# Single-bank PSUM tiles for the last batch, landing times in the planner, and token loads spread over the units

## The chip, the core and the metric

The kernel runs on one core of a Trainium2 chip. The metric is the device time of one execution in microseconds (us); the number quoted is the median of three runs. A profiled execution, taken apart from these runs, gives the trace. Engines are named as in the trace: PE (TensorE matmuls), PEld (its weight loads), DVE (VectorE), ACT (ScalarE), POOL (GpSimd), SP (SyncE, whose queue issues every DMA of this kernel; SPq in the rows).

## The reference

Three layers follow each other. Arrays are fp32.

```python
def _attn_ref(x, state):                     # x (4, 8, 512, 64), state (4, 8, 32, 64)
    scores = scale * np.matmul(x, state.transpose(0, 1, 3, 2))
    a = softmax(scores)                      # over the 32 state rows
    xread = np.matmul(a, state)
    a2 = softmax(scale * np.matmul(state, x.transpose(0, 1, 3, 2)))
    sread = np.matmul(a2, x)
    return np.concatenate([xread, sread], axis=2)

def _moe_ref(x, w_in, w_out):                # 2176 tokens, 512 -> 2048 -> 512
    h = x @ w_in
    g = np.where(h >= 1, h, np.where(h <= -1, 0.0, (h + 1) ** 2 / 4))
    return g @ w_out

def _moe2_ref(x, w_a, w_b, w_out):           # 512 -> 1536 -> 512
    return ((x @ w_a) * (x @ w_b)) @ w_out
```

(`softmax` stands here for the max, exp, sum and division of the reference.) The 2176 tokens are 4 batches of 512 and 128 state rows.

## The kernel before

**Arithmetic.** PE multiplies in a short format, so an fp32 operand is split into a high part, which ACT writes (a copy into `rh`, `r`, `r0` or `r1`), and a low part, which DVE writes (a subtraction, L356). Each product is then three passes: high by high, high by low, low by high. The three large matmuls (`g @ w_out`, the pair `x @ w_a`, `x @ w_b`, and the last one) are done with seven block products instead of eight, called by their numbers (in `b_steps` in the order 1, 2, 5, 3, 6, 7, 4). Sums of blocks are made by DVE (L900) before a product, and finished products are added up by ACT copies and DVE adds that read PSUM.

**Stages.** `phase_one` runs 64 units, t = 0 to 63: unit t is batch t // 16 and one slice of 128 of the 2048 middle columns. A unit is 6 matmuls of 512 columns into one PSUM bank (`h_mm`, L371), then its gate: ACT takes the ReLU out of the bank into an SBUF buffer `g` (L779), ACT or POOL squares it (L786, L788), DVE clamps it and so reads the bank a second time (L793), and SP stores it to DRAM, array `g_d` (L337). Between units 47 and 48 four groups of `h_state` matmuls (L825) do the state rows in the same way. The next stage, `b_steps`, multiplies `g` by `w_out`: it loads tokens of `g_d` back (L334, `f1<-g_d` and `f0<-g_d`, each 128x2x368), splits them and runs the seven products of each of three chunks of tokens, each product into two banks. Its first steps are taken between the last units, so that units and products are mixed there. `ab_run` then makes the two factors of the last layer (stored as `p_d`, L337), and `o_run` reads `p_d` back in pieces of 128x6x256 and makes the output, run after run.

**Banks.** PSUM has 8 banks of 512 fp32 words. Banks 0 to 3 are single tiles. Banks 4, 5 and banks 6, 7 are each one tile of 1024 words, because the attention's steps read both at once. The tile framework keeps its waits per tile, so an engine that reads bank 6 waits for a write of bank 7 before it in the program, and the other way round. Units 0 to 47 take banks 0 to 3 in turn (`four`), units 48 to 63 take 4, 5, 6, 7, 2, 3, again 4, 5, 6, 7, 2, 3, and then 6, 7, 2, 3 (`six`). In `b_steps` products 2 and 5 alone use banks 4 to 7, with product 3 adding onto product 5's banks 6 and 7. The buffers `g` of units 48 to 63 are a ring of six (`qlast`), so unit 54 writes the buffer of unit 48 once its store has landed.

**The order of the work.** One planner, `Flow`, puts the whole program in an order. Each operation has a cost per engine that may do it, its dependences, and for a transfer its size. `order()` walks through a modelled time: per step it takes the engine and the operation that can start first, PE's own in program order. `fin[i]` is when a result is usable; for a transfer it is when it lands (its share of one modelled wire and `DMA_LAT` behind it). `free[e]` is when the engine can issue its next operation. `when[s]`, the earliest start of a successor, is `free[e]` if both run on the same engine, else `fin[i]`. All transfers are on SP, so a load that reads what a store writes counts as ready once the store is issued, though on the chip SP waits there until it has landed, and every transfer behind it in the queue waits too. `STARTS` lists at which unit each of the first 17 steps of `b_steps` begins; the first 12 are the token loads of one piece each, which the line `flow.gate = units[-1]` ties to the unit before.

Of the kernel before, what the change touches and what calls it, by code (L numbers as in the profile page):

```python
# [9 lines left out]
F32 = mybir.dt.float32  # L10
F32R = mybir.dt.float32r
U32 = mybir.dt.uint32
AF = mybir.ActivationFunctionType
ALU = mybir.AluOpType
AX = mybir.AxisListType
PSUM = bass.MemoryType.PSUM
# [3 lines left out]
class Flow:  # L20
# [64 lines left out]
    def order(self):  # L85
        ops = self.ops
# [48 lines left out]
        for _ in range(n):  # L135
            best = None
            for e, f in free.items():
                x = None
                if e == "PE" and at < len(chain) and not left[chain[at]]:
                    i = chain[at]  # L140
                    x = (max(f, when[i]), 1e9, i, e)
                soon = min((max(f, when[i]) for i in ready[e]), default=0.0)
                soon += self.SOON if soon < self.EARLY else 0.0

                z = None
                for i in ready[e]:
                    t = max(f, when[i])
                    if t <= soon:
                        y = (late[i], t, i)
                        z = min(z, y) if z else y  # L150
                if z:
                    y = (z[1], z[0], z[2], e)
                    x = min(x, y) if x else y
                if x:
                    best = min(best, x) if best else x
            if best is None:

                raise RuntimeError("nothing is ready")
            t, _, i, e = best
            start[i] = t  # L160
            free[e] = t + ops[i][0][e]
            if i in self.port and e in shared:
                other = shared["POOL" if e == "DVE" else "DVE"]
                free[e] += min(max(other - t, 0.0), ops[i][0][e])
                shared[e] = free[e]
            if i in ideal:
                at += 1
                lag = max(lag, t - ideal[i])
            else:
                for x in ops[i][0]:  # L170
                    ready[x].remove(i)
            fin[i] = free[e] + self.LAT[e]
            if ops[i][3]:
                wire = max(wire, free[e]) + ops[i][3] / self.DMA_RATE
                fin[i] = wire + self.DMA_LAT
            for s in after[i]:
                left[s] -= 1
                when[s] = max(when[s], free[e] if (e,) == (*ops[s][0],) else fin[i])
                if not left[s]:
                    offer(s)  # L180
            self.ops[i] = (*ops[i][:4], e)
# [5 lines left out]
def attention_then_two_mlps(  # L187
# [28 lines left out]
    SWITCH = 48  # L216
    HOLD = 1
    FILL = (12, 10)
    STARTS = (48, 48, 49, 49, 50, 50, 51, 51, 52, 53, 54, 55, 56, 57, 59, 61, 62)
    HALVES = 1  # L220
    TIMES = ((0, 3, 4, 5), (8, 10, 12, 18), (22, 24, 26, 34), (38, 40, 42, 0))
    RUSH = (4, 8, 4, 4)
# [81 lines left out]
    def bank(b):  # L304
        return ("P", b, b + 1)
# [23 lines left out]
    def t_mm(n, passes=1):  # L329
        return passes * max(n / 2400 + 0.0135, 0.112)  # L330
# [30 lines left out]
        hi_of(hi, src, n, regs(src), regs(hi) + list(also))  # L361
        tt(lo, src, lambda: hi(F32), ALU.subtract, n, regs(src, hi), regs(lo))

    def mms(b, cols, pairs, first, last, n, rd, onto=False, off=0):


        def emit(e):
# [4 lines left out]
                    o, w, x, start=first and k == 0, stop=last and k == n - 1, skip_group_check=onto  # L372
                )

        return op({"PE": n * t_mm(cols)}, emit, rd, [bank(b)])

    def three(w, x):

# [70 lines left out]
    arenas["R0"] = pc.tile([P, RLO // 4], F32R, name="r0")  # L449
    arenas["F0"] = pc.tile([P, F0 // 4], F32, name="f0")  # L450
    banks = [ps.tile([P, 512], F32, name=f"bank{b}") for b in range(4)]
    lower, upper = (ps.tile([P, 1024], F32, name=f"bank{b}") for b in (45, 67))
    banks += [lower[:, :512], lower[:, 512:], upper[:, :512], upper[:, 512:]]
    both = [("P", 4, 6)]
    spare = pc.tile([P, 1], F32, name="spare")
    g_d = pd.tile([F1, P, T], F32, name="g_d")
# [79 lines left out]
    def b_soft(b):  # L536
# [9 lines left out]
                port=True,  # L546
            )

        op({"DVE": 1.25}, lambda e: nc.vector.transpose(t1(), lower), both, regs(t1))
        op({"DVE": 1.22}, lambda e: nc.vector.reduce_max(mx(), b32w(t1()), axis=AX.X), regs(t1), regs(mx))  # L550
        spread(ALU.subtract, mx)
        act(t1, t1, 1024, AF.Exp, regs(t1), regs(t1), scale=SCALE)
# [97 lines left out]
    def w_steps(b, n, f0=0, f1=4):  # L650
# [26 lines left out]
        for q in [range(2)] if WIDE and cols == 4 * P else [range(1), range(1, 2)]:  # L677
            k, at = len(q), wsum[n][q[0]][0].at + 4 * P * f0
            hi, lo = (V2("R0", at + 2048 * h, k, 1024, cols) for h in range(2))
            src = lambda q=q: upper.rearrange("p (q c) -> p q c", q=2)[:, q[0] : q[-1] + 1, :cols]  # L680
            held = [bank(6 + i) for i in q]
            steps.append(lambda hi=hi, src=src, held=held, k=k: hi_of(hi, src, k * cols, held, regs(hi)))
            steps.append(
# [6 lines left out]
    def s_soft(b):  # L690
# [1 line left out]
        a2, sm = d["a2"], d["sm"].sub(64, 16)  # L692
        op(
            {"DVE": 1.22},
            lambda e: nc.vector.reduce_max(sm()[:, 0:2], lower.rearrange("p (q c) -> p q c", q=2), axis=AX.X),
            both,
            regs(sm),
        )
# [36 lines left out]
    def s_tr(b):  # L735
        d = bs[b]
        for q in range(2):
# [5 lines left out]
                    nc.tensor.transpose(banks[4 + q][:, r], v()[:, r], ident)  # L743

            op({"PE": 0.5}, emit, regs(v), [bank(4 + q)], loose=True)
        act(d["a2t"], lambda: lower, 1024, AF.Copy, both, regs(d["a2t"]))

    def s_read(b):
        d = bs[b]
# [20 lines left out]
    four, six = Ring([0, 1, 2, 3]), Ring([4, 5, 6, 7, 2, 3] * 2 + [6, 7, 2, 3])  # L770

    begun = {}
    units, first_w = [], []

    def gate(b, g, put):
        h = lambda: banks[b]
# [22 lines left out]
    def h_mm(j, f, cs=range(2)):  # L799
# [7 lines left out]
            return out  # L807

        used = [v.sub(P * o, P) for q in cs for v in wsum[n][q]] + [v for q in cs for v in att[2 * j + q]]
        units.append(mms(b, 512, pairs, cs[0] == 0, cs[-1] == 1, 3 * len(cs), regs(*used)))  # L810
        if cs[-1] < 1:
            begun[j, f] = b
            return
# [679 lines left out]
    with tc.manual_schedule():  # L1493
        nc.vector.memset(half, 0.5)
        nc.scalar.activation(spare, half, AF.Exp)
        make_identity(nc, ident)
        pool = tc.tile_pool(name="fs", bufs=1)
        arenas["FS"] = pool.__enter__().tile([P, FSB // 4], F32, name="fs")
        for i in order:
            if i == first_rh[0]:  # L1500
                pool.__exit__(None, None, None)
                del arenas["FS"]
# [9 lines left out]
            flow.ops[i][1](flow.ops[i][4])  # L1512
        pool.__exit__(None, None, None)
        high.__exit__(None, None, None)


# [46 lines left out]
```

## Time and profile before

| | |
|---|---|
| median of 3 runs | 731.68 us (731.52 to 732.62) |
| profiled execution, its own time | 737.83 us |
| its span, first to last instruction | 735.0 us |
| PE busy / PEld busy | 706.0 us (96%) / 658.3 us |
| DVE / ACT / POOL busy | 554.6 / 422.2 / 104.7 us |
| mean granted TensorE clock | 0.991 |
| chain that ended last | PE 78%, DMA 9%, DVE 6%, ACT 3% |

A share of busy time is a mean over stages. Times in the rows below are microseconds from the start of the span; the profiled execution's time is its span and 2.83 us around it. In a row of a timeline the bracket is the idle time of the engine just ahead of the work, and whose work ended it.

### The profile page before, as it was taken

The page shows a single profiled execution, that of the slowest core. Times are in us where ns is not written, and L with a number is a line of the kernel's source. Part 1 is how long each engine was busy: PE and PEld are TensorE (multiplying, and loading weights), DVE is VectorE, ACT ScalarE, POOL GpSimd, SP SyncE. Part 2 cuts the span into 40 slices and gives each one's busy share as a digit, 9 for nine tenths or more (in the row PEclk, how much of TensorE's full clock was granted, in tenths as well). Part 3 has the DMA queues.
Part 4 walks back from the last instruction along what each step waited for, and adds up shares of the span by engine and source line. Part 5 has one row for each costly group of instructions (what it writes and reads, how often), then busy time and mean ns, then how long its engine had stood idle before and what let it go on. Part 6 is the DMA issues. An engine that isn't in the chain of part 4 may idle for free.

```text
span 735.0 us, 12233 instructions
## 1 busy us (share of the span) xinstructions
PE 706.0 (96%) x4818; PEld 658.3 (90%) x4818; DVE 554.6 (75%) x699; ACT 422.2 (57%) x623; POOL 104.7 (14%) x76
## 2 busy tenths in 40 slices
PE   7789899998999999999999999999999998999997
PEld 6356576987999999999999999999999998999997
DVE  6897769977898587789899786655636787978760
ACT  4787878777544445656566675655425445444440
POOL 3356546975000000000000000000000000000000
PEclk9999999999999999999999999999999999999999
DMA  9858867486557048125334767453541348345201
GB/s 344 355 196 274 312 210 279 145 302 212 183 189 280 21 122 253 57 85 173 100 122 169 261 186 241 154 176 132 190 147 41 109 140 274 101 146 171 85 33 43
DMA packets 75449, 128.92 MB, mean 175 GB/s; under 512 B 5632, under 2 KB 51200, under 8 KB 75392
## 3 DMA queue, kind: packets, MB, share of 16 engines
q1 hardware_dynamic: 75392, 128.15, 52.0%
q8 instruction: 37, 0.61, 0.3%
q14 instruction: 20, 0.16, 0.1%
HBM read 84.87 MB, written 43.25 MB: 174 GB/s over the span
## 4 chain that ended last, share of the span: by engine, by line
PE 78%; DMA 9%; DVE 6%; ACT 3%; issue 2%; POOL 1%; SPq 1%; ACTq 0%; POOLq 0%; DVEq 0%
PE bank L371 73%; DMA f<-in_w_dram 4%; PE bank L825 2%; DMA p_d<-f 1%; DMA f<-p_d 1%; ACT f L346 1%; DMA f<-g_d 1%; DVE r L356 1%; DMA g_d<-f 1%; PE bank L758 1%; DVE rh L356 1%; PE bank L660 1%; PE bank L849 1%; DVE fs L434 1%; DVE f L793 1%
## 5 line engine op out<-in xcount | busy, mean ns | idle before, releaser
L371 PE MATMUL bank<-rh,r 128*128 128x352 f32 (+2 forms) x1398 | 225.0, 316 | 4.8 <-ACT f L346 3.8
L371 PEld LDWEIGHTS bank<-rh,r 128*128 128x128 f32 x1398 | 216.2, 189 | 8.0 <-ACT f L346 5.9
L371 PE MATMUL bank<-r,r 128*128 128x368 f32 (+1 forms) x960 | 158.1, 317 | 3.5 <-ACT f L346 3.4
L346 ACT ACTIVATE f<-bank 128x368 f32<-128x368 f32 (+3 forms) x183 | 82.2, 453 | 130.4 <-PE bank L371 129.7
L371 PEld LDWEIGHTS bank<-r,r 128*128 128x128 f32 x960 | 149.4, 190 | 4.2 <-ACT f L346 4.2
L346 ACT ACTIVATE rh<-f 128x736 fp32r<-128x736 f32 (+4 forms) x120 | 100.4, 846 | 77.5 <-PE bank L371 62.1
L356 DVE TENSOR_TENSOR f<-bank,f 128x368 f32<-128x368 f32 (+2 forms) x168 | 85.8, 517 | 73.9 <-PE bank L371 63.8
L356 DVE TENSOR_TENSOR rh<-f,rh 128x736 fp32r<-128x736 f32 (+5 forms) x120 | 115.5, 973 | 27.5 <-ACT rh L346 27.1
L371 PE MATMUL bank<-r 128*128 128x512 f32 (+1 forms) x582 | 124.3, 366 | 7.6 <-DVE fs L793 2.8
L371 PEld LDWEIGHTS bank<-r 128*128 128x128 f32 x582 | 96.6, 193 | 35.0 <-issue 7.1
L356 DVE TENSOR_TENSOR r<-f,r 128x768 fp32r<-128x768 f32 (+6 forms) x85 | 94.1, 1114 | 20.9 <-ACT r L346 20.7
L346 ACT ACTIVATE r<-f 128x768 fp32r<-128x768 f32 (+6 forms) x85 | 80.2, 952 | 39.6 <-PE bank L371 19.0
L371 PE MATMUL bank<-rh 128*128 128x352 f32 (+2 forms) x564 | 93.4, 318 | 0.5 <-DVE f L356 0.5
L900 DVE TENSOR_TENSOR f<-f 128x256 f32<-128x256 f32 (+7 forms) x107 | 85.7, 817 | 6.8 <-issue 3.0
L371 PEld LDWEIGHTS bank<-rh 128*128 128x128 f32 x564 | 88.4, 189 | 1.6 <-issue 0.7
L371 PE MATMUL bank<-r,rh 128*128 128x368 f32 (+1 forms) x480 | 80.3, 315 | 0.0
L371 PEld LDWEIGHTS bank<-r,rh 128*128 128x128 f32 x480 | 74.3, 188 | 0.0
L346 ACT ACTIVATE f<-f 128x1024 fp8e5<-128x1024 f32 (+1 forms) x43 | 47.8, 1119 | 2.8 <-POOL f L423 2.6
L421 ACT ACTIVATE f<-f 128x512 fp8e5<-128x512 fp8e5 (+1 forms) x29 | 29.5, 1017 | 25.3 <-DMA f<-in_w_dram 20.1
L434 DVE SCALAR_TENSOR_TENSOR f<-f 128x1024 uint32<-128x1024 uint32 (+1 forms) x34 | 35.7, 1050 | 6.3 <-ACT f L346 6.1
L793 DVE SCALAR_TENSOR_TENSOR f<-f,bank 128x512 f32<-128x512 f32 x40 | 26.5, 677 | 14.0 <-POOL f L788 5.3
L779 ACT ACTIVATE f<-bank,half 128x512 f32<-128x512 f32 x40 | 26.9, 687 | 15.2 <-PE bank L371 8.1
(64 smaller groups left out, 430.0 us busy)
## 6 DMA issues: line engine op xcount, KB each, us to landing
f<-in_w_dram SPq DMA_DIRECT2D x25, 1024.0 KB, 6.5
f<-g_d SPq DMA_DIRECT2D x36, 368.0 KB, 4.7
f<-p_d SPq DMA_DIRECT2D x17, 768.0 KB, 4.9
g_d<-f SPq DMA_DIRECT2D x40, 256.0 KB, 4.6
f<-in_w_dram SPq DMA_DIRECT2D x18, 512.0 KB, 3.9
p_d<-f SPq DMA_DIRECT2D x48, 184.0 KB, 2.1
g_d<-fs SPq DMA_DIRECT2D x28, 256.0 KB, 3.8
f<-g_d SPq DMA_DIRECT2D x16, 352.0 KB, 4.6
```

Source lines behind the costliest of these rows:

```text
L346: lambda e: nc.scalar.activation(dst(), src(), func, **{k: (v() if callable(v) else v) for k, v in kws.items()}),
L356: op({"DVE": t_tt(n)}, lambda e: nc.vector.tensor_tensor(dst(), a(), b(), alu), rd, wr, port=port)
L371: nc.tensor.matmul(o, w, x, start=first and k == 0, stop=last and k == n - 1, skip_group_check=onto)
L421: nc.scalar.activation(to(), of(), AF.Copy, saturate=False)
L434: lambda e: nc.vector.scalar_tensor_tensor(out(U32), words_of(1, U32)(), 5, z(U32), ALU.logical_shift_right, ALU.bitwise_or),
L660: nc.tensor.matmul(banks[ab[q]][o : o + NS, :cols].rearrange("p (f x) -> p f x", x=P), st[q]()[64 * h : 64 * h + 64, NS * j : NS * j + NS] ...
L758: nc.tensor.matmul(banks[4][64 * e2 : 64 * e2 + 64, o : o + NS], xn()[:, c * 256 + p * 128 + e2 * 64 : c * 256 + p * 128 + (e2 + 1) * 64], ...
L779: lambda e: nc.scalar.activation(g(), h(), AF.Relu, bias=half[:, 0:1], scale=0.5),
L793: lambda e: nc.vector.scalar_tensor_tensor(g(), g(), 1.0, h(), ALU.min, ALU.max),
L825: nc.tensor.matmul(banks[b][:, P * i : P * i + P], w[:, P * c : P * c + P], xs()[:, P * c : P * c + P], start=c == 0, stop=c == 3,)
L849: nc.tensor.matmul(banks[3][:, :128], ident, ident, start=True, stop=True)
L900: lambda e: eng(e).tensor_tensor(dst(), a(), b(), alu),
```

## The change

It has three parts.

1. In `Flow.order` the earliest start of a successor on the same engine is `free[e]` only if the operation ahead is no transfer; behind a transfer it is its landing.
2. `STARTS`: from unit 50 on the token loads start at one per unit, where before they started at two per unit up to unit 51.
3. The tiles of two banks live until unit 48 alone (`SWITCH`). There their pool closes, and a pool of four tiles of one bank each takes their place for the rest of the program. Unit 48's matmuls count for the planner as a write of banks 4 to 7.

```diff
@@ Flow.order
-                when[s] = max(when[s], free[e] if (e,) == (*ops[s][0],) else fin[i])
+                when[s] = max(when[s], free[e] if (e,) == (*ops[s][0],) and not ops[i][3] else fin[i])
@@
-    STARTS = (48, 48, 49, 49, 50, 50, 51, 51, 52, 53, 54, 55, 56, 57, 59, 61, 62)
+    STARTS = (48, 48, 49, 49, 50, 51, 52, 53, 54, 55, 56, 57, 57, 58, 59, 61, 62)
@@ mms
-        return op({"PE": n * t_mm(cols)}, emit, rd, [bank(b)])
+        return op({"PE": n * t_mm(cols)}, emit, rd, [bank(b), *also])
@@ the tiles
-    lower, upper = (ps.tile([P, 1024], F32, name=f"bank{b}") for b in (45, 67))
-    banks += [lower[:, :512], lower[:, 512:], upper[:, :512], upper[:, 512:]]
+    banks += [None] * 4
+    wide = {}
@@ h_mm
+        also = ()
+        if 16 * j + f == SWITCH:
+            also = [("P", 4, 8)]
+            narrow.append(len(flow.ops))
+        units.append(mms(b, 512, pairs, cs[0] == 0, cs[-1] == 1, 3 * len(cs), regs(*used), also=also))
@@ where the program is written out
+        both_banks = tc.tile_pool(name="pw", bufs=1, space=PSUM)
+        opened = both_banks.__enter__()
+        for name, b in (('lower', 4), ('upper', 6)):
+            wide[name] = opened.tile([P, 1024], F32, name=name)
+            banks[b : b + 2] = [wide[name][:, :512], wide[name][:, 512:]]
...
         for i in order:
+            if i == narrow[0]:
+                both_banks.__exit__(None, None, None)
+                both_banks = tc.tile_pool(name="pn", bufs=1, space=PSUM)
+                opened = both_banks.__enter__()
+                banks[4:] = [opened.tile([P, 512], F32, name=f"bank{b}") for b in range(4, 8)]
```

What this does to the order is seen at two places. **The last batch, SP.** The rows are transfers in the order in which SP issues them, from the stores of the `h_state` groups on; `g_d` is the array in DRAM, `f0` and `f1` are arenas in SBUF, a store of 128x4x128 is an `h_state` group, one of 128x512 a unit from 48 on, a load of 128x2x368 one piece of tokens. Before:

```order
L337 DMA g_d_74<-f0_66 128x4x128
L334 DMA f0_66<-g_d_74 128x2x368 x2
L337 DMA g_d_74<-f0_66 128x4x128
L334 DMA f0_66<-g_d_74 128x2x368 x2
L334 DMA f1_1265<-g_d_74 128x2x368 x2
L337 DMA g_d_74<-f0_66 128x4x128
L334 DMA f1_1265<-g_d_74 128x2x368 x3
L337 DMA g_d_74<-f0_66 128x512 x2
L334 DMA f1_1265<-g_d_74 128x2x368
L337 DMA g_d_74<-f0_66 128x512
L334 DMA f1_1265<-g_d_74 128x2x368 x2
L337 DMA g_d_74<-f0_66 128x512 x5
```

With the change:

```order
L337 DMA g_d_72<-f0_66 128x4x128 x2
L334 DMA f0_66<-g_d_72 128x2x368 x3
L337 DMA g_d_72<-f0_66 128x4x128
L334 DMA f1_1275<-g_d_72 128x2x368
L334 DMA f0_66<-g_d_72 128x2x368
L334 DMA f1_1275<-g_d_72 128x2x368
L337 DMA g_d_72<-f0_66 128x512
L334 DMA f1_1275<-g_d_72 128x2x368
L337 DMA g_d_72<-f0_66 128x512 x2
L334 DMA f1_1275<-g_d_72 128x2x368 x3
L337 DMA g_d_72<-f0_66 128x512 x2
L334 DMA f1_1275<-g_d_72 128x2x368 x2
```

Ahead of unit 48's store stood nine loads, and now stand six; ahead of unit 49's stood nine, and now seven; ahead of unit 50's ten, and now seven.

**The last batch, PE.** The rows are PE's matmuls from units 58 and 59 (`bank2`, `bank3`) to units 60 and 61, the second use of banks 6 and 7, with the pass over one piece of tokens of product 1 (`bank0`, `bank1`) between them. Before:

```order
L371 MATMUL bank2_69<-r0_65 128x512 [waits DVE_49]
L371 MATMUL bank2_69<-r0_65 128x512 x5
L371 MATMUL bank3_70<-r0_65 128x512 [waits DVE_49]
L371 MATMUL bank3_70<-r0_65 128x512 x5
L371 MATMUL bank0_67<-rh_1261,r0_65 128x368 [waits Activation_49]
L371 MATMUL bank0_67<-rh_1261,r0_65 128x368 [waits DVE_49]
L371 MATMUL bank0_67<-rh_1261,r0_65 128x368 x4
L371 MATMUL bank1_68<-rh_1261,r0_65 128x368 x6
L371 MATMUL bank67_72<-r0_65 128x512 [waits DVE_49]
L371 MATMUL bank67_72<-r0_65 128x512 x11
```

With the change (`bank6_1257` and `bank7_1258` are the new tiles):

```order
L371 MATMUL bank3_70<-r0_65 128x512 [waits DVE_49]
L371 MATMUL bank3_70<-r0_65 128x512 x5
L371 MATMUL bank0_67<-rh_1271,r0_65 128x368 [waits Activation_49]
L371 MATMUL bank0_67<-rh_1271,r0_65 128x368 [waits DVE_49]
L371 MATMUL bank0_67<-rh_1271,r0_65 128x368 x4
L371 MATMUL bank1_68<-rh_1271,r0_65 128x368 x6
L371 MATMUL bank6_1257<-r0_65 128x512 [waits DVE_49]
L371 MATMUL bank6_1257<-r0_65 128x512 x5
L371 MATMUL bank7_1258<-r0_65 128x512 [waits DVE_49]
L371 MATMUL bank7_1258<-r0_65 128x512 x5
```

One wait for both halves of a tile has become a wait per bank. Unit 58 is not in these rows any more, since it now stands ahead of the piece of product 1 before them, and unit 57 ahead of the one before that.

**The output stage, ACT.** The rows are ACT's operations where `o_run`'s first and second runs meet: `f0<-bank` copies a finished product out of PSUM, `r1<-f0`, `r0<-f0` and `rh<-f0` are the high parts of operands. Before:

```order
L346 ACTIVATE f0_66<-bank3_70 128x512 [waits PE_49]
L346 ACTIVATE r1_2842<-f0_66 128x768 [waits DMAHW7_49]
L346 ACTIVATE f0_66<-bank0_67 128x256 [waits PE_49]
L346 ACTIVATE r0_65<-f0_66 128x768 [waits DVE_49]
L346 ACTIVATE f0_66<-bank45_71 128x256 [waits PE_49]
L346 ACTIVATE rh_1261<-f0_66 128x768 [waits DMAHW5_49,Activation_49]
```

With the change:

```order
L346 ACTIVATE f0_66<-bank3_70 128x512 [waits PE_49]
L346 ACTIVATE f0_66<-bank0_67 128x256 [waits PE_49]
L346 ACTIVATE r0_65<-f0_66 128x768 [waits DVE_49]
L346 ACTIVATE f0_66<-bank5_1256 128x256 [waits PE_49]
L346 ACTIVATE rh_1271<-f0_66 128x768 [waits DMAHW5_49,Activation_49]
L346 ACTIVATE r1_2853<-f0_66 128x768 [waits DMAHW7_49]
```

The operand that waits for a load (`DMAHW7`) stood ahead of two copies out of banks, and now stands behind them. SP's order of the loads and stores around it is the same in both.

## Rows read from the trace of the kernel before

**Rows 1.** The page, parts 1 and 6: engines, and issues to landing (median us).

```profile
PE 706.0 (96%) x4818; PEld 658.3 (90%) x4818; DVE 554.6 (75%) x699; ACT 422.2 (57%) x623; POOL 104.7 (14%) x76
...
g_d<-f SPq DMA_DIRECT2D x40, 256.0 KB, 4.6
```

**Rows 2.** Waits of PE, 182 to 735 us: us in total, times, longest.

```profile
PE bank L371 <- ACT f L346: 7.2, 8, 3.4
```

**Rows 3.** Windows: length, busy time of PE, PEld, DVE, ACT, POOL, PEclk, DMA.

```profile
170.00:176.00 6.00, 4.61 (x14) 3.78 (x15) 4.92 (x6) 3.30 (x7) 2.11 (x1) 0.74 0.76 244
195.00:200.00 5.00, 3.87 (x22) 3.25 (x21) 2.73 (x3) 2.40 (x4) 0.00 (x0) 1.00 0.94 320
...
612.00:622.00 10.00, 6.63 (x43) 6.54 (x43) 6.83 (x7) 5.98 (x9) 0.00 (x0) 0.83 1.09 362
...
300.00:350.00 50.00, 47.84 (x291) 46.48 (x291) 43.56 (x52) 30.58 (x45) 0.00 (x0) 1.00 0.31 104
```

**Rows 4.** Timeline of PE, last batch: start, us, engine, line, count, idle before.

```profile
164.11 2.89 PE L371 MATMUL bank<-r 128*128 128x512 f32 x12
166.84 2.18 PE L371 MATMUL bank<-rh,r 128*128 128x368 f32 x12
171.39 4.21 PE L371 MATMUL bank<-r 128*128 128x512 f32 x12 [2.37 <-DVE f L793]
175.40 2.60 PE L371 MATMUL bank<-rh,r 128*128 128x368 f32 x12
```

**Rows 5.** Timeline of ACT, last batch.

```profile
163.92 1.33 ACT L779 ACTIVATE f<-bank,half 128x512 f32<-128x512 f32 x2 [2.15 <-DMA g_d<-f]
166.22 0.69 ACT L779 ACTIVATE f<-bank,half 128x512 f32<-128x512 f32 x1 [0.96 <-DMA g_d<-f]
...
168.78 1.32 ACT L779 ACTIVATE f<-bank,half 128x512 f32<-128x512 f32 x2 [0.50 <-DMA g_d<-f]
```

**Rows 6.** Timeline of DVE, last batch.

```profile
170.65 1.29 DVE L793 SCALAR_TENSOR_TENSOR f<-f,bank 128x512 f32<-128x512 f32 x2 [0.17 <-ACT f L786]
171.85 1.81 DVE L900 TENSOR_TENSOR f<-f,f 128x1472 f32<-128x1472 f32 x1
```

**Rows 7.** Timeline of SP's issues, last batch.

```profile
149.34 0.36 SPq L337 DMA_DIRECT2D g_d<-f  x1
151.64 1.92 SPq L334 DMA_DIRECT2D f<-g_d  x4
...
156.41 1.37 SPq L337 DMA_DIRECT2D g_d<-f  x2
```

**Rows 8.** Timeline of PE, output stage.

```profile
615.47 6.05 PE L371 MATMUL bank<-r,r 128*128 128x256 f32 x36 [3.37 <-ACT f L346]
621.35 4.42 PE L371 MATMUL bank<-rh,r 128*128 128x256 f32 x36
```

**Rows 9.** Timeline of all engines from 613.5 us.

```profile
614.30 0.84 ACT L346 ACTIVATE r<-f 128x768 fp32r<-128x768 f32 x1 [5.38 <-DMA f<-p_d]
615.05 0.36 ACT L346 ACTIVATE f<-bank 128x256 f32<-128x256 f32 x1
615.17 0.96 DVE L356 TENSOR_TENSOR r<-f,r 128x768 fp32r<-128x768 f32 x1 [4.03 <-ACT r L346]
```

**Rows 10.** Timeline of SP's issues, output stage.

```profile
604.28 0.64 SPq L337 DMA_DIRECT2D p_d<-f  x1
609.62 1.55 SPq L334 DMA_DIRECT2D f<-p_d  x3
```

**Rows 11.** Timeline of all engines from 196.6 us, products 5 and 3.

```profile
196.93 0.48 ACT L346 ACTIVATE f<-bank 128x368 f32<-128x368 f32 x1 [1.19 <-PE bank L371]
...
197.46 1.28 PE L371 MATMUL bank<-rh,r 128*128 128x368 f32 x6 [0.57 <-ACT f L346]
198.77 0.48 ACT L346 ACTIVATE f<-bank 128x368 f32<-128x368 f32 x1 [1.37 <-PE bank L371]
...
199.30 0.44 PE L371 MATMUL bank<-rh,r 128*128 128x368 f32 x1 [0.57 <-ACT f L346]
```

More of the change, by code (lines that the diff above doesn't have):

```diff
@@ L362, in split, with mms @@
         tt(lo, src, lambda: hi(F32), ALU.subtract, n, regs(src, hi), regs(lo))
-    def mms(b, cols, pairs, first, last, n, rd, onto=False, off=0):
+    def mms(b, cols, pairs, first, last, n, rd, onto=False, off=0, also=()):
         def emit(e):
@@ L547, in spread @@
             )
-        op({"DVE": 1.25}, lambda e: nc.vector.transpose(t1(), lower), both, regs(t1))
+        op({"DVE": 1.25}, lambda e: nc.vector.transpose(t1(), wide["lower"]), both, regs(t1))
         op({"DVE": 1.22}, lambda e: nc.vector.reduce_max(mx(), b32w(t1()), axis=AX.X), regs(t1), regs(mx))
@@ L679, in w_steps @@
             hi, lo = (V2("R0", at + 2048 * h, k, 1024, cols) for h in range(2))
-            src = lambda q=q: upper.rearrange("p (q c) -> p q c", q=2)[:, q[0] : q[-1] + 1, :cols]
+            src = lambda q=q: wide["upper"].rearrange("p (q c) -> p q c", q=2)[:, q[0] : q[-1] + 1, :cols]
             held = [bank(6 + i) for i in q]
@@ L694, in s_soft @@
             {"DVE": 1.22},
-            lambda e: nc.vector.reduce_max(sm()[:, 0:2], lower.rearrange("p (q c) -> p q c", q=2), axis=AX.X),
+            lambda e: nc.vector.reduce_max(sm()[:, 0:2], wide["lower"].rearrange("p (q c) -> p q c", q=2), axis=AX.X),
             both,
@@ L745, in s_tr @@
             op({"PE": 0.5}, emit, regs(v), [bank(4 + q)], loose=True)
-        act(d["a2t"], lambda: lower, 1024, AF.Copy, both, regs(d["a2t"]))
+        act(d["a2t"], lambda: wide["lower"], 1024, AF.Copy, both, regs(d["a2t"]))
     def s_read(b):
@@ L772, in attention_then_two_mlps @@
     begun = {}
-    units, first_w = [], []
+    units, first_w, narrow = [], [], []
     def gate(b, g, put):
@@ L809, in h_mm @@
         used = [v.sub(P * o, P) for q in cs for v in wsum[n][q]] + [v for q in cs for v in att[2 * j + q]]
-        units.append(mms(b, 512, pairs, cs[0] == 0, cs[-1] == 1, 3 * len(cs), regs(*used)))
+        also = ()
[3 more added lines that the diff above has]
+        units.append(mms(b, 512, pairs, cs[0] == 0, cs[-1] == 1, 3 * len(cs), regs(*used), also=also))
         if cs[-1] < 1:
@@ L1514, in attention_then_two_mlps @@
         high.__exit__(None, None, None)
+        both_banks.__exit__(None, None, None)
 def kernel(**inputs):
```

## The prediction

> **What bounds the kernel now.** I read the engine table of the page first: PE is busy for 706.0 us of the span and no other engine is near it [rows 1]. So the end moves only where PE stands still, or where its matmuls take longer than elsewhere. The second view is PE's list of waits. Behind the units it names little but ACT's copies out of PSUM: 7.2 us in 8 waits, the longest 3.4 [rows 2]. The third is PE's timeline, read for idle time in brackets and for rows of the same matmuls with different durations. Three places come out of it that the change touches.
>
> *Place A, the last batch.* At 171.39 PE has waited 2.37 us for a clamp of DVE [rows 4]. The 12 matmuls behind the wait take 4.21 us, where the same 12 took 2.89 at 164.11, and the next 12 take 2.60, where they took 2.18 at 166.84. In the window around it the granted clock is 0.74; its two levels are 1.2 and 2.4 GHz, and the stretch lies partly at the lower one [rows 3]. The place costs 2.37 + 1.32 + 0.42 = 4.11 us.
>
> Why was DVE late? Units 60 and 61 write banks 6 and 7 again and need the clamps of units 56 and 57, which run as a pair at 170.65 [rows 6]. ACT's reading ahead of them stood still three times, 2.15, 0.96 and 0.50 us, for stores of `g_d` [rows 5]: the ring of six buffers was full, since unit 54 needs the buffer of unit 48. The stores of units 48 and 49 went out at 156.41 [rows 7]. SP had been taken up with token loads, and the first of a group of them, at 151.64, went out 2.30 us after the store at 149.34.
>
> *Place B, the output stage.* PE waits 3.37 us until 615.47 for ACT's copy of bank 0, and the 36 matmuls behind take 6.05 us where the next 36 take 4.42 [rows 8]; the window's clock is 0.83 [rows 3]. That is 3.37 + 1.63 = 5.00 us. ACT stood for 5.38 us at the split ahead of that copy, which waits for a load of `p_d` [rows 9]; the load went out only at 609.62, 5.34 us after the store that it reads [rows 10].
>
> *Place C, products 5 and 3 of `b_steps`.* PE waits 0.57 us at 197.46 and again at 199.30 [rows 11]. ACT's copy of bank 6 began when the whole product was through, the one of bank 7 only after PE's next 6 matmuls, into bank 6. The pair comes once in each of three chunks, so six times 0.57, 3.42 us. It fits the list of waits: 7.2 less the 3.4 of place B leaves 3.8 for seven waits [rows 2].
>
> **The planner's landing times.** The rule adds and removes no instruction; it moves. At place A it takes three loads from ahead of the stores of units 48 and 50, and two from ahead of unit 49's. Four loads take 1.92 us to issue, 0.48 each [rows 7], so the stores go out 1.0 to 1.4 us earlier by that alone; where SP's 2.30 us of standing also falls away, 3.7. What is needed is that the clamps come 2.37 us earlier. Two things give it together: ACT's three waits on stores, 3.61 us in all [rows 5], of which 1.0 to 3.6 go, and the tiles, below. I take all 2.37, and with it the 1.74 of slow matmuls. What is late next is DVE: a sum of 1472 values, 1.81 us [rows 6], that waits for token loads and stands ahead of clamps; it has the difference 3.61 − 2.37 = 1.24 us to spare.
>
> At place B the load is now known to be late, so the planner puts the split behind two copies and another split. The copy of bank 0 goes when its product is done, and PE goes on at 615.47 − 3.37 = 612.10. The 36 matmuls of products 6 and 3 take some 4.3 us, to 616.4. The next product needs the late operand: landed by 614.30, 0.84 on ACT and 0.96 on DVE give 616.1 [rows 9]. It is just in time, and 5.00 us is the gain, less what is missing there. If the load lands 1 us later, about 0.7 comes back.
>
> **The token loads, one per unit.** They are the same loads of the same size; pieces from unit 50 on are tied to a unit up to two later. They are what clears SP ahead of the stores, so their gain is in the sum of A. Their cost is nothing so long as product 1's pieces wait between units for PE; without that cover a load that is late by one unit holds PE for up to the length of its 6 matmuls, 1.45 us (half of 2.89 [rows 4]).
>
> **The single banks.** At A, unit 60 no longer needs unit 57's clamp, so its bank is free one clamp earlier, 0.65 us (half of 1.29 [rows 6]). With the stores only 1.0 us earlier, 0.7 of the wait stays; at 1.7 or more nothing does. At C, bank 6's last 6 matmuls end some 1.1 us ahead of bank 7's (the half of 2.18 [rows 4]), and the copy with its release took 0.53 us to PE's start, 196.93 to 197.46 [rows 11]. It is hidden, and so is bank 7's behind the next six. All 3.42 go. Closing one pool and opening another adds a wait to unit 48's first matmul alone, on readings of the attention that are done by then; I cost it at nothing. A few operations change engines in front of unit 48: a low half of 1024 values and a sum go from POOL to DVE. PE runs the `h_state` groups there; uncovered it would be some 1.8 us by the nearest row [rows 6].
>
> **A rule of the skill that weighs here.** At C, PE pauses shortly and often, and in the window around it the granted clock stays at 1.00 [rows 3]; at A and B one longer wait each was followed by slow matmuls. The Trainium skill, TensorE: Matmul & The Clock Gate, in its section on depth-cycling of the PSUM queue, says that cycling through banks with frequent very short idle times can make the clock swing between its levels. By that rule C would have cost six times the 1.74 us of A on top, and the change would bring 10.4 us more; by the row it brings 3.42. I go by the row.
>
> **The sum.** A 4.11 + B 5.00 + C 3.42 = 12.53 us. Both ends: nothing given back is 12.5; in a stretch like 300 to 350 DVE is busy for 43.56 of 50 us [rows 3], so the third chunk may give back its 1.1, and B may miss 0.7. I take 1.0 off, an estimate between those, and reach 11.5. Against the profiled execution's own time that is 737.83 − 11.5 = 726.3, a factor of 0.9844. That execution stood 6.15 us above the median of the runs; carried over by the factor, the median becomes 731.68 × 0.9844 = 720.3 us.
>
> **Rivals.** (All relative to 720.3.) Changes of up to 0.2%, about 1.5 us, can't be told from none.
>
> 1. *A stays.* The 1472-word sum, or a store that lands late (4.6 us in the median [rows 1]), keeps the clamps back. For it: only 1.24 us to spare. Against it: one wait per bank. 720.3 + 4.1 = 724.4 us.
> 2. *B stays.* The load, still behind the same store, lands 2 us or more later, and the wait and the slow matmuls move to the next product. For it: SP's order there is unchanged. Against it: nothing moves the store either. 720.3 + 5.0 = 725.3.
> 3. *The clock.* More waits, each for one bank, make PE pause at every unit of the last batch, and all units run as slowly as those behind the wait of A: 1.32 us more per 12 matmuls [rows 4], 0.66 per unit of 6, 10.6 for 16 units: 730.9. Against it: the clock at C. This is the section named above, with the sign turned.
> 4. *No change.* The waits move on: DVE, now unhindered, is late everywhere after, and A, B and C come back as waits for DVE. 731 us. Against it: DVE is 554.6 of 735 [rows 1].
> 5. *Slower.* A load that waits for a landing holds SP, and with it each later store. Three links of `h_state` store and load stand ahead of unit 48; if each holds the chain of gates by what the load of `p_d` took, 5.3 us [rows 10], PE loses 16 us against a gain of 11.5: 736. It decides from (11.5 + 1.5) / 3 = 4.3 us per link on. Against it: the one such wait in the last batch was 2.3 us [rows 7] and was partly covered.
>
> **Chances.** Forecast 0.60; rival 1 0.14; rival 2 0.10; rival 3 0.02; rival 4 0.05; rival 5 0.05; more than 12.5 us, from waits that I did not count, 0.04. The forecast's own range is 718.5 to 722.5. The range of 8 in 10 takes in rivals 1 and 2 and, below, a gain of 15: 716.8 to 725.5. Faster by over 0.2%: 0.60 + 0.14 + 0.10 + 0.04 = 0.88; within: 0.02 + 0.05 = 0.07; slower: 0.05.
>
> **What would show it.** In the profile after: no wait of PE for a clamp between 165 and 175 us and a granted clock near 1.00 there; ACT's ReLUs of units 54 to 57 without idle time for `g_d`; unit 48's store ahead of 155 us. In the output stage ACT's copy right behind product 2, PE's next wait there under 1 us. At C no waits of 0.57. The prediction is wrong if PE's busy time falls short of the same work elsewhere, if a new wait stands between 146 and 183 us, or if the wait at B reappears one product on.

## The result and the profile after

The changed kernel takes 720.11 us (median of 4 runs, 718.84 to 724.56), before 731.7 us (4 runs): a ratio of 0.985, 95% interval 0.9806 to 0.9894. Its profiled execution took 719.44 us, 717.3 of them span. The page's engine table answers to [rows 1], the waits of PE behind the units to [rows 2]:

```profile
span 717.3 us, 12235 instructions
...
PE 699.2 (97%) x4818; PEld 655.4 (91%) x4818; DVE 559.3 (78%) x701; ACT 424.8 (59%) x625; POOL 97.3 (14%) x72
```

```profile
PE bank L371 <- DVE rh L356: 2.1, 3, 0.8
PE bank L371 <- ACT f L346: 0.5, 1, 0.5
PE bank L371 <- DVE f L356: 0.5, 1, 0.5
```

Of the 7.2 us of waits for ACT one of 0.5 is left. Waits for low parts on DVE are up to 2.1 us in three, of which two, of 0.75 and 0.76 us, are new. In the same list before stood:

```profile
PE bank L371 <- DVE rh L356: 0.9, 2, 0.6
```

The windows, as in [rows 3], show the clock at its upper level at A and where B was:

```profile
144.00:183.00 39.00, 39.00 (x202) 35.35 (x201) 34.83 (x34) 33.05 (x46) 20.87 (x12) 1.00 0.80 271
...
600.00:612.00 12.00, 11.95 (x102) 11.74 (x101) 9.44 (x11) 7.61 (x11) 0.00 (x0) 1.00 0.98 323
```

PE's timeline in and behind the last batch answers to [rows 4]. The change's program is 4 us earlier here, for a reason that is no part of it (D, below), so rows are found by their work, not by their time:

```profile
164.88 2.89 PE L371 MATMUL bank<-r 128*128 128x512 f32 x12
167.60 2.18 PE L371 MATMUL bank<-rh,r 128*128 128x368 f32 x12
169.62 1.53 PE L371 MATMUL bank<-r 128*128 128x512 f32 x6
...
185.60 2.28 PE L371 MATMUL bank<-rh,r 128*128 128x368 f32 x12 [0.75 <-DVE rh L356]
188.64 3.63 PE L371 MATMUL bank<-rh,r 128*128 128x368 f32 x20 [0.76 <-DVE rh L356]
```

The pass over tokens ends and the next units start without a wait; the two new waits come 16 us later. ACT's ReLUs have one wait for a store left, of 0.25 us, where [rows 5] had 3.61; unit 48's store went out at 147.69, before at 156.41 (3.9 of these 8.7 us are the shift of the program):

```profile
154.60 0.69 ACT L779 ACTIVATE f<-bank,half 128x512 f32<-128x512 f32 x1 [0.25 <-DMA g_d<-f]
```

```profile
147.69 0.51 SPq L337 DMA_DIRECT2D g_d<-f  x1
148.25 0.44 SPq L334 DMA_DIRECT2D f<-g_d  x1
148.78 1.12 SPq L337 DMA_DIRECT2D g_d<-f  x2
```

In the output stage, PE's timeline and ACT's, for [rows 8] and [rows 9]:

```profile
597.36 6.56 PE L371 MATMUL bank<-r,r 128*128 128x256 f32 x54
603.75 4.73 PE L371 MATMUL bank<-rh,r 128*128 128x256 f32 x36
```

```profile
597.74 0.37 ACT L346 ACTIVATE f<-bank 128x256 f32<-128x256 f32 x1
...
602.22 0.85 ACT L346 ACTIVATE r<-f 128x768 fp32r<-128x768 f32 x1 [3.38 <-DMA f<-p_d]
```

The 54 matmuls of three products run through. ACT still waits 3.38 us for the same load, but the copy out of bank 0, at 597.74, stands ahead of it.

**Where the time went.** PE runs the same 4818 matmuls in every kernel of this study, so the time from the start of one to the start of another, by their number, can be laid side by side. The stretches: D, matmuls 628 to 660, in the units near 88 us, which the change doesn't touch; A, 1115 to 1245; N, 1300 to 1356, in the products behind A; C, 1356 to 1380, 1690 to 1720 and 2000 to 2050 together; B, 3860 to 3900; tail, 4600 to 4650. In us, one profiled execution each:

```
                                    D       A       N       C       B    tail
before                          10.92   30.67    9.40   22.12    9.88    6.39
after                            7.09   26.43   11.51   17.12    4.73    5.95
landing                          8.03   28.60    9.86   21.67    4.73    6.39
STARTS                           6.86   27.96    9.40   21.67   11.32    6.39
tiles                            6.89   26.47   10.98   17.12    9.76    5.95
tiles + landing                  7.66   28.53   10.16   17.11    4.73    5.95
landing + STARTS                 7.67   27.96    9.40   21.64    4.73    6.40
tiles + STARTS                   7.09   26.43   10.58   17.11   11.36    5.95
new order, two-bank waits        7.27   29.36   11.52   22.14    4.73    6.40
old order, single-bank waits     8.06   27.31    9.40   17.12   10.94    5.95
after, last operands in halves  10.37   26.43   10.12   17.12    4.73    5.95
after, low parts on POOL         8.24   26.43   21.80   18.61    4.73    5.95
after, sums on DVE               7.83   26.43    9.40   17.12    4.73    5.95
after, sums on DVE and halves    8.00   26.43    9.40   17.11    4.73    5.95
```

From before to after: A 4.24, C 5.00, B 5.15 and the tail 0.44 us won, N 2.11 lost, and elsewhere 1.21 won; 13.9 us in all. The tail is a fourth place of the two-bank tiles: a wait of 0.21 us for DVE that is there in each kernel with two-bank waits and in none without. D's 3.83 is no part of the change: up to there the order is the same on every engine in all of these kernels, and PE waits for a clamp that hangs on the landing of a weight load. The wait was 2.77 us in the profile before and 0.57 after, and in the others 0.32 to 2.25. If D in the median run of the kernel before is as in most of the others, 7 to 8 us, it makes some 3 to 4 of the 6.15 us by which the profiled execution before stood above the median; no profile of a median run shows it. What is left between 13.9 and the 11.6 of the medians isn't placed. Without D and elsewhere, the stretches give 12.7 us here, and in the runs below they agree with the medians within 2.2 us, save for the tiles alone.

### The profile page after: what moved, and what is told of

It reads as the page before. It is cut to its first block, busy times and chain, and to the rows that moved or that the text cites. A ratio compares the mean times of both kernels' runs of the same rounds, so it can differ in the third digit from the quotient of the medians.

```text
span 717.3 us, 12235 instructions
## 1 busy us (share of the span) xinstructions
PE 699.2 (97%) x4818; PEld 655.4 (91%) x4818; DVE 559.3 (78%) x701; ACT 424.8 (59%) x625; POOL 97.3 (14%) x72
## 4 chain that ended last, share of the span: by engine, by line
PE 82%; DVE 7%; DMA 5%; ACT 2%; issue 2%; POOL 1%; SPq 0%; DVEq 0%; POOLq 0%; ACTq 0%
PE bank L371 76%; DMA f<-in_w_dram 2%; PE bank L829 2%; DVE rh L356 2%; DMA p_d<-f 1%; DMA f<-p_d 1%; PE upper L660 1%; DVE r L356 1%; PE lower L758 1%; PE bank L853 1%; ACT f L346 1%; DVE fs L434 1%; DVE fs L549 1%; DVE fs L793 1%; ACT rh L346 0%
## 5 line engine op out<-in xcount | busy, mean ns | idle before, releaser
L371 PE MATMUL bank<-r,r 128*128 128x368 f32 (+1 forms) x960 | 156.1, 315 | 0.0
L371 PEld LDWEIGHTS bank<-r,r 128*128 128x128 f32 x960 | 147.9, 188 | 0.0
L346 ACT ACTIVATE rh<-f 128x736 fp32r<-128x736 f32 (+5 forms) x120 | 100.7, 846 | 77.7 <-PE bank L371 61.3
L356 DVE TENSOR_TENSOR rh<-f,rh 128x736 fp32r<-128x736 f32 (+5 forms) x120 | 120.2, 1014 | 26.1 <-ACT rh L346 25.6
L371 PE MATMUL bank<-r 128*128 128x512 f32 (+1 forms) x582 | 122.1, 362 | 2.8 <-ACT r L346 1.1
L356 DVE TENSOR_TENSOR r<-f,r 128x768 fp32r<-128x768 f32 (+6 forms) x85 | 91.9, 1090 | 15.7 <-ACT r L346 15.6
```

Source lines behind the costliest of these rows:

```text
L346: lambda e: nc.scalar.activation(dst(), src(), func, **{k: (v() if callable(v) else v) for k, v in kws.items()}),
L356: op({"DVE": t_tt(n)}, lambda e: nc.vector.tensor_tensor(dst(), a(), b(), alu), rd, wr, port=port)
L371: nc.tensor.matmul(o, w, x, start=first and k == 0, stop=last and k == n - 1, skip_group_check=onto)
```

## The experiments

The first three take over one part of the change each, the next three leave one out.

**Landing times alone.**

```diff
-                when[s] = max(when[s], free[e] if (e,) == (*ops[s][0],) else fin[i])
+                when[s] = max(when[s], free[e] if (e,) == (*ops[s][0],) and not ops[i][3] else fin[i])
```

> Only the planner's landing times are taken over; STARTS and the two-bank tiles stay as before. Theory (each place has its own part): the wait at B goes, since the copy of bank 0 again stands ahead of the operand that waits for the load, and with it the slow matmuls behind: 5 us. C stays whole (six waits of 0.57 us). At A eight loads instead of nine stand ahead of unit 48's store and the wait for both halves of a tile stays: at most 1.5 us there. Together 725.5 us (724.5 to 727). Rival (the landing times alone cure A too, because SP no longer stands for a store): 5 + 4 = 9 us, 722.5 us, and no wait of PE for a clamp near 171 us.

724.75 us, 0.991 (0.9874 to 0.9946): the theory's time. B is gone, C is there, with one wait of 0.93 us in place of the first pair. Nine loads, not eight, still stand ahead of unit 48's store (the last five of them in SP's rows below), but SP stands less between them. At A ACT has no wait for a store left, but PE waits all the same, in its timeline (SP's rows stand behind it):

```profile
168.78 1.65 PE L371 MATMUL bank<-r 128*128 128x512 f32 x6 [1.43 <-DVE f L793]
```

```profile
148.22 2.92 SPq L334 DMA_DIRECT2D f<-g_d  x5
151.24 1.16 SPq L337 DMA_DIRECT2D g_d<-f  x2
```

Stores in time are not enough for A.

**STARTS alone.**

```diff
-    STARTS = (48, 48, 49, 49, 50, 50, 51, 51, 52, 53, 54, 55, 56, 57, 59, 61, 62)
+    STARTS = (48, 48, 49, 49, 50, 51, 52, 53, 54, 55, 56, 57, 57, 58, 59, 61, 62)
```

> Only STARTS is taken over. Theory: seven instead of nine loads stand ahead of unit 48's store, which goes out 1 to 2 us earlier, but units 60 and 61 still wait for the clamps of units 56 and 57 together: of A 1 to 2.5 us go, B and C stay. 730 us (729 to 731). Rival (the loads were all of A): the wait of 2.37 us and the slow matmuls go, 727.5 us. Second rival (STARTS only starves product 1): 732.5 us or more, with waits of PE for rh between 158 and 183 us.

730.46 us, 0.999 (0.9965 to 1.0015). The profile has A 2.7 us shorter, with a wait of 1.19 us left at 154 us, and B longer in this execution (a wait of 3.64 us). Product 1 isn't starved. In the time this can't be told from no change.

**Tiles alone.** The edit is the change's part 3 without the lines of the other two.

> Only the single-bank tiles are taken over. Theory: all six waits at C go, 4.7 us by the starts of the matmuls (1.56 per pair, more than the 1.14 of idle time in the rows); at A unit 60 waits for one clamp instead of two, which takes about 0.7 to 1.5 us off the wait; B stays whole. 726 us (725 to 727.5). Rival (the pair of halves was the whole of A): A goes as well, 722.5 us, no wait of PE for a clamp near 171 us.

726.46 us, 0.9932 (0.9903 to 0.996). The time is the theory's, and C is gone and B is there, as it said. But the rival was right about A: in the profiled execution, which took 724.40, PE has no wait there (26.47 us in the table), although ACT's timeline still shows the stores late by 3.06 us in all, nearly the 3.61 of [rows 5]:

```profile
159.97 1.27 ACT L779 ACTIVATE f<-bank,half 128x512 f32<-128x512 f32 x2 [1.49 <-DMA g_d<-f]
163.46 2.06 ACT L779 ACTIVATE f<-bank,half 128x512 f32<-128x512 f32 x3 [1.00 <-DMA g_d<-f]
169.17 0.69 ACT L779 ACTIVATE f<-bank,half 128x512 f32<-128x512 f32 x1 [0.57 <-DMA g_d<-f]
```

So the theory's time came without its wait at A, as far as one profile shows. The stretches add up to 8.2 us and the median gained 5.0; its seven runs lie at 724.1 to 724.5 and at 726.5 to 728.7, and what parts them isn't known. N has lost 1.58 us here already.

**Tiles and landing, old STARTS.** The changed kernel with the line above taken back.

> The changed kernel with the old STARTS. Theory: B and C are gone, A is left in part: 721.5 us (720 to 723). Rival (STARTS does nothing once the other two are there): the same time as the changed kernel, 720.1 us within 0.7, and no wait of PE for a clamp near 171 us. Second rival (STARTS costs something by itself, the two waits of PE for a low part near 186 and 189 us): faster than the changed kernel, 718.5 us, without these two waits.

720.68 us, 0.9855 (0.982 to 0.9889): in the theory's range, and no difference to the changed kernel that can be measured. PE's timeline has the theory's wait at A, and at N one wait of 0.49 us in place of the changed kernel's two:

```profile
168.51 1.67 PE L371 MATMUL bank<-r 128*128 128x512 f32 x6 [1.78 <-DVE f L793]
...
183.67 6.64 PE L371 MATMUL bank<-rh,r 128*128 128x368 f32 x38 [0.49 <-DVE rh L356]
```

DVE's timeline shows what stood ahead of the clamp: two sums over token loads, which start without a wait, then a clamp waiting for POOL's square.

```profile
163.55 3.29 DVE L904 TENSOR_TENSOR f<-f,f 128x1472 f32<-128x1472 f32 x2
167.77 1.88 DVE L793 SCALAR_TENSOR_TENSOR f<-f,bank 128x512 f32<-128x512 f32 x3 [0.93 <-POOL f L788]
```

So STARTS takes 2.1 us from A, and N takes 1.35 of them back (10.16 to 11.51). But N isn't STARTS' doing: it is longer by 0.8 to 2.1 us in the five kernels of the table that have an order planned with the single-bank tiles (the changed one, tiles alone, tiles with either other part, and the new order with two-bank waits), and by 0 to 0.5 in the four others that keep the old planning at unit 48.

**Landing and STARTS, no tiles.** Both one-line edits on the kernel before.

> The changed kernel with the two-bank tiles kept and planned for as before: landing times and STARTS without the tiles. Theory (the pair of halves makes A, the stores alone don't cure it): B is gone, C's six waits stand, and one wait of PE for a clamp of 1 to 2 us is left between 150 and 175 us, even though ACT no longer waits for stores there. 724 us (723 to 726). Rival (stores that go out in time are enough): no wait for a clamp, 722 us.

724.69 us, 0.9898 (0.9866 to 0.9929): the theory. C is there, again with one wait of 0.93 us in place of the first pair, B is gone, and PE's timeline keeps one wait at A (ACT does wait for stores here, 1.15 and 0.63 us):

```profile
155.19 3.04 PE L371 MATMUL bank<-r 128*128 128x512 f32 x12 [1.21 <-DVE f L793]
```

**Tiles and STARTS, old rule for transfers.** The changed kernel with the landing edit taken back.

> The changed kernel with the planner's old rule for transfers. Theory: B is there whole (a wait of 3.3 to 3.6 us for ACT's copy near 603 us and slow matmuls behind), C is gone, A is gone as with the tiles alone. 726 us (724.5 to 727.5). Rival (A needs the landing times): a wait for a clamp of over 1 us between 150 and 175 us, 727.5 us or more.

725.39 us, 0.9908 (0.9877 to 0.994): the theory. B is there (a wait of 3.73 us), A and C are gone. N has one wait, ahead of where the changed kernel has its two:

```profile
183.71 16.54 PE L371 MATMUL bank<-rh,r 128*128 128x368 f32 x97 [0.91 <-DVE rh L356]
```

B belongs to the landing rule alone: with it 4.73 us in every profile, without it 9.76 to 11.36.

**The new order with two-bank waits.** What separates the tiles from the order that the planner finds with them:

```diff
-            if i == narrow[0]:
-                both_banks.__exit__(None, None, None)
-                both_banks = tc.tile_pool(name="pn", bufs=1, space=PSUM)
-                opened = both_banks.__enter__()
-                banks[4:] = [opened.tile([P, 512], F32, name=f"bank{b}") for b in range(4, 8)]
```

> The changed kernel's order word for word, but the tiles of two banks are kept to the end, so that the waits are again for both halves. Theory (C and what is left of A come from the waits, not from the order): C's six waits of about 0.57 us are back, worth 4.7 us by the starts of the matmuls, and PE waits 0.5 to 2 us for a clamp where units 60 and 61 write banks 6 and 7 again; B stays gone. 725.5 us (724 to 727). Rival (the order that the planner found does it): 720 to 721.5 us, without these waits.

728.62 us, 0.9954 (0.9936 to 0.9972): slower than the theory's range. A lost more than forecast, 2.93 us, with two waits instead of one, and C and the tail lost 5.47. Four of its waits in PE's timeline, two at A and the pair of the second chunk:

```profile
156.38 1.67 PE L371 MATMUL upper<-r 128*128 128x512 f32 x6 [1.45 <-DVE f L793]
...
169.04 1.67 PE L371 MATMUL upper<-r 128*128 128x512 f32 x6 [0.85 <-DVE f L793]
...
252.51 1.28 PE L371 MATMUL upper<-rh,r 128*128 128x368 f32 x6 [0.57 <-ACT f L346]
254.36 3.96 PE L371 MATMUL upper<-rh,r 128*128 128x368 f32 x22 [0.57 <-ACT f L346]
```

C's six waits, of 0.55 to 0.57 us, are back and cost 5.02 us, 0.84 each. The order is the changed kernel's on every engine.

**The old order with single-bank waits.** The mirror: the changed kernel with both one-line edits taken back, and without the line that tells the planner of unit 48's write of banks 4 to 7. The order is that of the kernel before on all engines.

```diff
-            also = [("P", 4, 8)]
```

> The mirror of the run with the changed kernel's order and two-bank waits: the order of the kernel before word for word on every engine, with single-bank tiles from unit 48 on, so that only the waits differ. Theory (the waits for both halves make C and the larger part of A, even with the old order): C's six waits go (5.0 us by the starts of the matmuls), and A's matmuls from unit 52 on take 27 to 28.5 us instead of 30.7, with ACT still waiting for the stores; B stays. 724.5 us (723 to 726.5). Rival (at A the late stores hold PE in this order, whatever the tiles): PE still waits over 1 us for a clamp near 171 us, and the time is 727.5 us.

724.40 us, 0.9892 (0.9859 to 0.9924): the theory. PE's timeline and ACT's at A:

```profile
167.81 1.65 PE L371 MATMUL bank<-r 128*128 128x512 f32 x6 [0.59 <-DVE f L793]
```

```profile
160.48 1.26 ACT L779 ACTIVATE f<-bank,half 128x512 f32<-128x512 f32 x2 [1.87 <-DMA g_d<-f]
162.59 0.69 ACT L779 ACTIVATE f<-bank,half 128x512 f32<-128x512 f32 x1 [0.84 <-DMA g_d<-f]
165.16 1.36 ACT L779 ACTIVATE f<-bank,half 128x512 f32<-128x512 f32 x2 [0.52 <-DMA g_d<-f]
```

The stores are late by 3.23 us in all, and of PE's 2.37 us of waiting 0.59 is left, and none of the slow matmuls. In the old order the tiles are worth 3.36 us at A (30.67 to 27.31), in the new one 2.93; the new order adds 0.9.

**The new waits at N.** Four runs on the changed kernel. First, DVE's long instructions cut in two:

```diff
-        for k in ((0, 8),):
+        for k in parts:
             v_split(i, *k, {"3": vq(1, *k, 0), "6": vq(0, *k, 0), "7": vq(0, *k, 1)}[i])
```

> The changed kernel, with the last three operands of w_out split in halves of 1024 values instead of 2048 at once. Theory (the two waits of 0.75 us near 185.6 and 188.6 us, new in the changed kernel, are for low parts that stand on DVE behind instructions of 2.3 us): they shrink to under 0.3 us each, 1 to 2 us less, 718.7 us (717.5 to 719.8). Rival (DVE is full there whatever the size): the waits stay or move, and the added fixed cost of three instructions on DVE and ACT leaves 720 us or more.

720.02 us, 0.9833 (0.9803 to 0.9863). Of N's 2.11 us 1.39 are gone, and one wait is left:

```profile
185.83 14.38 PE L371 MATMUL bank<-rh,r 128*128 128x368 f32 x84 [0.43 <-DVE rh L356]
```

A wait for DVE of 0.72 us comes up at 218 us, and D was 10.37 in this profile. The time tells nothing apart, and the edit also changed which of DVE's work stands beside POOL's. Second, the low parts offered to POOL:

```diff
-        tt(rows(lo), src, rows(hi, F32), ALU.subtract, n, regs(src, hi), regs(lo))
+        op(
+            {x: t_tt(n) if x == "DVE" else 0.2 + 0.0019 * n for x in engs},
+            lambda e: eng(e).tensor_tensor(rows(lo)(), src(), rows(hi, F32)(), ALU.subtract),
+            regs(src, hi), regs(lo), port=True,
+        )
...
-            v_split(i, *k, {"3": vq(1, *k, 0), "6": vq(0, *k, 0), "7": vq(0, *k, 1)}[i])
+            v_split(i, *k, {"3": vq(1, *k, 0), "6": vq(0, *k, 0), "7": vq(0, *k, 1)}[i], engs=BOTH)
```

> The changed kernel, with the low parts of the last three operands of w_out open to POOL as well; the planner puts three of 2048 values on POOL. Theory (the new waits near 185.6 and 188.6 us come from DVE's long instructions): both go, 2.0 us less by the starts of the matmuls, and products 6 and 7 don't come later: 718.2 us (717 to 719.5). Rival (POOL's long instructions slow DVE, or come too late for product 6): waits of PE for DVE of 1 us or more between 180 and 215 us, 720 us or more.

730.71 us, 0.9984 (0.9963 to 1.0005): the rival, and far past it; the gain of the whole change is gone. POOL's, DVE's and PE's timelines:

```profile
174.93 4.75 POOL L900 TENSOR_TENSOR r<-f,r 128x2048 fp32r<-128x2048 f32 x1 [6.24 <-PE bank L371]
180.85 6.07 POOL L910 TENSOR_TENSOR f<-f 128x1024 f32<-128x1024 f32 x2 [1.16 <-DVE r L900]
186.84 10.73 POOL L900 TENSOR_TENSOR r<-f,r 128x2048 fp32r<-128x2048 f32 x2
```

```profile
175.14 5.63 DVE L900 TENSOR_TENSOR r<-f,r 128x1024 fp32r<-128x1024 f32 x1
...
181.53 0.67 DVE L793 SCALAR_TENSOR_TENSOR f<-f,bank 128x512 f32<-128x512 f32 x1
...
188.22 5.00 DVE L900 TENSOR_TENSOR rh<-f,rh 128x1024 fp32r<-128x1024 f32 x1
193.14 6.88 DVE L356 TENSOR_TENSOR rh<-f,rh 128x736 fp32r<-128x736 f32 x3
```

```profile
198.41 1.90 PE L371 MATMUL bank<-rh,r 128*128 128x368 f32 x5 [8.37 <-DVE rh L356]
```

While POOL does two subtractions, DVE's of 1024 values takes 5.00 us instead of 1.2, and PE waits 8.37 us. With that in view, POOL's and DVE's timelines of the changed kernel:

```profile
176.27 5.46 POOL L904 TENSOR_TENSOR f<-f 128x1024 f32<-128x1024 f32 x2 [7.80 <-DVE r L356]
```

```profile
176.04 1.28 DVE L793 SCALAR_TENSOR_TENSOR f<-f,bank 128x512 f32<-128x512 f32 x2
177.45 5.06 DVE L356 TENSOR_TENSOR rh<-f,rh 128x736 fp32r<-128x736 f32 x2
...
187.68 2.58 DVE L356 TENSOR_TENSOR rh<-f,rh 128x736 fp32r<-128x736 f32 x3
```

The clamps, which read a bank, take their 0.64 us each beside POOL; the low parts, with both inputs in SBUF, take 5.06 for two where three take 2.58 later. They end at 182.51 us, 0.78 behind the end of POOL's second sum at 181.73. In the run with the low parts on POOL, DVE's subtraction of 1024 values ends at 180.77, 1.09 behind POOL's at 179.68. Since alone they take 0.91 and 1.22, they don't seem to run slower, but to stand until POOL's instruction is over and run then. All eleven low parts beside POOL's sums or subtractions, in the changed kernel and three of these runs, end 0.78 to 1.09 us behind a POOL instruction. The third run takes three sums away from POOL, the fourth adds the halves:

```diff
-            v_sum(vq(0, *k, 0), vq(1, *k, 0), vq(0, *k, 0), ALU.subtract, BOTH)
+            v_sum(vq(0, *k, 0), vq(1, *k, 0), vq(0, *k, 0), ALU.subtract, BOTH if k[0] == 0 else ("DVE",))
```

(the same for the two other sums that follow a split).

> The changed kernel, with three sums of 1024 values of the second half of w_out on DVE, which the planner may otherwise give to POOL. Its PE order is that of the changed kernel. In the changed kernel two of them run on POOL from 176.3 us for 5.5 us, and the two low parts on DVE beside them take 5.06 us where such a pair takes 1.75. Theory (the two new waits of PE near 185.6 and 188.6 us are for low parts that POOL holds up): DVE's low parts take 0.9 us each there, both waits go, 2.0 us less by the starts of the matmuls: 718 us (716.8 to 719.3). Rival (the waits come from DVE's own long instructions of 2.3 us ahead of the low parts): the waits stay at 0.5 us or more each, 720 us or more, since DVE has three instructions of 1.2 us more to do.

> As the run before with the sums on DVE, and the low and high parts of the last three operands of w_out in halves of 1024 values. Theory (POOL alone makes the waits): no difference to the run with the sums alone, 718 us, within 0.8. Rival (long instructions on DVE count as well): 0.7 to 1.5 us faster than that run, 717 us, where that run still shows waits of PE for DVE between 180 and 190 us.

718.79 us, 0.9839 (0.9809 to 0.9869), and 719.05 us, 0.9836 (0.9806 to 0.9866). In the third N is at 9.40, as before the change, and DVE's low part beside its own sums takes its 0.92:

```profile
176.77 2.48 DVE L904 TENSOR_TENSOR f<-f 128x1024 f32<-128x1024 f32 x2
179.16 0.92 DVE L356 TENSOR_TENSOR rh<-f,rh 128x736 fp32r<-128x736 f32 x1
```

Both waits are gone, with DVE's long instructions still in place: POOL made them. A wait of 0.49 us for DVE came up at 215 us instead. The halves add nothing. The median is 1.3 us under the changed kernel's, less than these runs can tell.

## Why the prediction was right, point by point

**The sum.** 12.53 us before give-back, 11.5 after it, was forecast; the medians moved by 11.6, the profiles without D by 13.9. The time is right partly by luck: two misses cancel in the sum, C 1.58 too small and the give-back 1.11 too small. The tail's 0.44 wasn't in it.

**Place A: the size right, the cause half right.** 4.11 us forecast, 4.24 measured. The step that failed is "Two things give it together: ACT's three waits on stores" and the tiles. The stores were not needed: with the tiles alone A is as short as in the changed kernel, though ACT waits 3.06 us for stores. They are not enough either: with the landing times alone ACT doesn't wait, and PE waits 1.43 us. That rule also takes no load from ahead of unit 48's store by itself, where the prediction gave it three. The tiles' term, 0.65 us, was sized from one clamp. With the order unchanged it measured 30.67 − 27.31 = 3.36 us, 1.78 of it waiting.

**Place B as forecast.** 5.00 us forecast, 5.15 measured, by the step named: the copy ahead of the operand that waits for the load. The operand came just in time; at most 0.3 us came back (4.73 us for the 36 matmuls from 603.75 on, where 4.42 is usual [rows 8]). Where the wait at B is left, its cost varies between executions, 9.76 to 11.36 us for the stretch.

**Place C: right mechanism, undersized term.** All six waits went, by the tiles alone. The "six times 0.57, 3.42 us" measured 5.00: a pause costs more at the starts of the matmuls, 0.83 us, than its idle time, which the profile counts from a modelled end.

**The rule on the clock.** Its answer for C would have been 10.4 us more; the six waits cost 5.0 in all. In the run that brings them back they come again at the same price, and the granted clock in its window of 190 to 198 us, with two of them, is 1.00. The Trainium skill, TensorE: Matmul & The Clock Gate, tells in its section on depth-cycling of the PSUM queue of another kernel whose clock swung; at C in this one the trace shows no such swing.

**The give-back.** One us was put on DVE in the third chunk and on B. It was 2.11 us, at N, and the third chunk gave nothing back. The step "A few operations change engines in front of unit 48", covered there by the `h_state` groups, looked at the wrong place: two of POOL's sums now follow a split that comes later, and run where DVE makes low parts instead of clamps. The Trainium skill has the mechanism, in SBUF — State Buffer, among the rules on its two sides: DVE and GpSimd share a pair of ports, locked for a whole instruction, against a DVE operation with two SBUF inputs if the GpSimd one reads SBUF. The trace agrees: beside POOL's sums two low parts take 5.06 us and end 0.78 behind POOL, and the clamps, which read PSUM, take their usual 0.64 each.

**STARTS.** Put down as what clears SP for A; in the changed kernel it is worth 2.1 us at A, and N takes 1.35 of them back; the medians, 720.68 without it and 720.11 with it, can't be told apart. Of rival 1, the sum ahead of the clamps is what DVE's rows show with the old STARTS. But it isn't load-bound there: the sums start without a wait, as the one of [rows 6] did.

## What to carry to other kernels

In this tile framework a tile that spans two banks makes each half's reader wait for the other half's writer, so look for pairs of short waits at the ends of accumulations; here each wait of 0.57 us cost 0.8. A planner that takes a transfer as done when it is issued puts work that waits for a load ahead of work that doesn't; the cure is in the order, and adds no instruction. When operations move, look at which instructions then run beside each other on POOL and DVE, not only at how long each takes.

## What the runs showed of the hardware

A subtraction of 2048 values on POOL (4.75 us in the run with the low parts there) stretched DVE's of 1024 values beside it from 1.2 to 5.63 us, by making it stand until POOL was through. Of the longer waits of PE, those of 1.43, 1.45 and 1.78 us at A were followed by matmuls at their usual pace and a granted clock of 1.00 in their window. Those of 2.37 us at A, 2.25 and 2.77 at D, 3.26 to 3.73 at B and 8.37 at N in the run with the low parts on POOL were followed by slow ones. In PE's timeline the first row is D in the changed kernel, the second D in the run with the operands in halves:

```profile
88.45 4.37 PE L371 MATMUL bank<-r 128*128 128x512 f32 x18 [0.57 <-DVE fs L793]
```

```profile
89.49 5.97 PE L371 MATMUL bank<-r 128*128 128x512 f32 x18 [2.25 <-DVE fs L793]
```

The 18 matmuls behind the longer wait take 1.6 us more. The wait at D hangs on when a DMA lands: ahead of it POOL's copy stood 4.17 us for a weight load in the profile before and 1.96 in the one after. With the same order of work, the stretch D took 6.86 to 10.92 us in the 14 profiled executions, the slow matmuls included.
